# A transformer block in float32: the tensor operations of GpSimd in the MLP phase go to VectorE, and the last tile pair takes three chunk pairs by the classical product

## The chip, the core and the metric

The kernel runs on one core of a Trainium2 chip. The metric is the device time of one execution in microseconds; where several executions are shown, their median counts. Besides the times there is a profile of one execution, taken by the hardware profiler, with a start and a duration for every instruction of every engine: PE (TensorE, matrix products), DVE (VectorE), ACT (ScalarE), POOL (GpSimd) and SP (SyncE, which here only starts transfers). Every engine works through its own queue strictly in the order in which the program was written; a waiting instruction holds up all that stand behind it.

## The reference

A block of a transformer works on 2048 tokens of width 640, in float32:

```python
mod = (silu(c) @ w_mod).reshape(1, 6, 1, 640)          # sa, ca, ga, sb, cb, gb
h = layernorm(x) * (1 + ca) + sa
x = x + ga * attention(h)                              # linear attention, 32 heads of 20
h = layernorm(x) * (1 + cb) + sb
u = h @ w1 + b1                                        # 640 -> 1728
x = x + gb * (max(u, 0) ** 2 @ w2 + b2)                # 1728 -> 640
```

The change concerns the last three lines, the MLP.

## The kernel before

**Numbers in two parts.** TensorE multiplies in a reduced format (`F32R` in the code, `fp32r` in the profile). To keep float32 accuracy every operand is split into a high part (a copy on ScalarE into the reduced format) and a low part (what is left, a subtraction on VectorE, in the helper `lo`, line 87), and a product of two operands takes three matrix products: high by high, high by low, low by high (the helper `three`). So every new operand costs a copy on ScalarE, then a subtraction on VectorE, before its third product can run.

**Tiles and chunks of the MLP.** 16 tiles of 128 tokens form 8 tile pairs, `j` from 0 to 7. The 1728 hidden features are 14 chunks of 128 (the last has 64), which form 7 chunk pairs, `n` from 0 to 6. For each `j` and each `n` there are two half steps. In the first `up(j, 2n)` computes an even chunk of hidden features, in the second `up(j, 2n+1)` the odd one: 15 matrix products into one half of the PSUM bank `UP` (10 for the last chunk). ScalarE applies the relu with the bias (line 1148, tile `ft`), VectorE squares it (line 1149). For the last chunk of 64 features the parts are put together in another way: ScalarE takes one part out of PSUM (line 1152), VectorE adds the other straight from PSUM (`L1153`) and squares (`L1154`). The next `up(j+1, 0)` begins the bank `UP` anew, so it waits until `L1153` has read it.

**The second product, one chunk pair late.** After each `up` stands half of the second product of the chunk pair before (`down(0)`, then `down(1)`), which sums into the PSUM banks `acc`, `acc3x`. The output is cut into 384 columns (left) and 256 columns (right). A chunk pair can be taken in two ways:

- classically (`down_plain`): four blocks of activations (two tiles by two chunks) by two column parts, that is 24 matrix products, 12 of 384 and 12 of 256 columns;
- as a Strassen-Winograd product (`down_pair`): seven block products in place of eight, that is 21 matrix products, 12 of 384 and 9 of 256 columns. It needs sums of the activation blocks (`sums`, four VectorE subtractions and additions of 128x128 on line 1163, split in `split_s` into the tile `rs`) and sums of the weights.

`plain(j, n)` tells which is used: classical for the tile pairs 0 and 1 (`PLAIN`), for the last chunk pair, and for the last two chunk pairs of the last tile pair.

**Sums of the weights.** For the chunk pairs 0 to 5 they are made once, while the tile pairs 1 and 2 run: `t_load` brings two rows of weights (tile `traw`), `t_sums` (line 1225) makes five subtractions, of which two are on GpSimd (128x256 and 128x128) and three on VectorE (128x256), `t_split` splits the results and writes them to memory (`td_a`, `td_b`, `td_c`). From then on `t_fetch` brings them back for every tile pair and chunk pair into the tiles `ring_a`, `ring_b`, `ring_c`; these transfers are started by GpSimd. One of the sums stays in place of the right part of `W2[2n]`; the last tile pair loads and splits the true right part for the chunk pair that it takes classically (`w10_load`, `w10_split`).

**The end of a tile pair.** `first_combos` and `end` put the output `y` together from the banks, `gate` multiplies by `gb`, and `finish` adds the residual `xr` and stores (VectorE and SyncE). The residual is loaded by `residual`, and the bias `bb` (128x640) is added to it by `add_bias` on GpSimd (line 1304), for both tiles of a pair one after the other: in the first chunk pair step of the next tile pair, for pair 1 in the third, for pair 7 in its own sixth. For the last tile pair, GpSimd also adds `xr` to `y` (line 1464) and makes two of the four last additions in `last_downs` (line 1359).

**The next tile pair.** `layer(j+1, at)` runs the layer norm of the next tile pair beside all this, at the half steps in the tables `LN_AT...`: `load_x1` loads two parts (`xm`, `xx`), `add_x` adds them (VectorE, line 974), `ln_pieces` takes mean and variance (ScalarE, with `xx` as scrap space, line 1381), and `t2` transposes on TensorE (`tb`), scales on ScalarE (`hfb`) and splits into `h` on ScalarE and VectorE.

**What sets the order.** For the MLP the order of PE, DVE, ACT and POOL is the order in which the loop is written (`by_hand`). SyncE's transfers are ordered by a scheduler; a transfer waits in SyncE's queue until its source is ready and its target free, and those behind it wait too. The tiles `traw`, `xr`, `xx` share five buffers (`s1`) in rotation, so a load waits for the reader of the tile five loads before.

Of the kernel before, what the change touches and what calls it, by code (L numbers as in the profile page):

```python
# [8 lines left out]
F32 = mybir.dt.float32  # L9
# [29 lines left out]
PLAIN = 2  # L39
W_AT = (  # L40
# [10 lines left out]
def kernel(  # L51
# [1104 lines left out]
    def plain(j, n):  # L1156
        return j < PLAIN or n == NF // 2 - 1 or j == NB - 1 and n == NF // 2 - 2

# [54 lines left out]
    def t_sums(n):  # L1213
# [8 lines left out]
        for eng, o, x, y in ((nc.vector, a[:, l], a[:, r], a[:, l]), (nc.gpsimd, t[:, 1].bitcast(F32), b[:, r], a[:, r]),  # L1222
                             (nc.vector, b[:, r], b[:, r], a[:, l]), (nc.gpsimd, b[:, m], b[:, m], a[:, m]),
                             (nc.vector, b[:, l], b[:, l], b[:, r])):
            eng.tensor_tensor(o, x, y, op=ALU.subtract)
# [17 lines left out]
    def w10_load():  # L1243
        TR_["w10"] = row("s1", "w10")
        f = NF - 4
        nc.sync.dma_start(TR_["w10"][:, R], w2[f * P : (f + 1) * P, R])

    def w10_split():

        t, w = W2[NF - 4][:, :, R], TR_["w10"][:, R]  # L1250
        nc.scalar.activation(t[:, 0], w, AF.Copy)
        lo(t[:, 1], w, t[:, 0])
# [34 lines left out]
    def down_pair(j, n, part):  # L1287
        v, w = W2[2 * n], W2[2 * n + 1]
        last = n == NF // 2 - 2 - (j == NB - 1)
# [12 lines left out]
    def add_bias(j):  # L1302
        for i in range(2):
            nc.gpsimd.tensor_tensor(XR[j, i], XR[j, i], bb, op=ALU.add)
# [39 lines left out]
    def last_downs(j):  # L1344
# [3 lines left out]
        for regs in ((("3", 0, R), ("x", 1, R)), (("2", 0, L),), (("4", 1, L),)):  # L1348
# [4 lines left out]
            for r, i, c in regs:  # L1353
# [4 lines left out]
                eng = nc.gpsimd if r in "x2" else nc.vector  # L1358
                eng.tensor_tensor(Y[j][i][:, c], Y[j][i][:, c], t, op=ALU.add)
# [11 lines left out]
    LN_AT1 = {"load": 3, "add": (5, 5), "ln": (5, 6, 6, 7, 8, 8), 9: (0, 1), 10: (2, 3), 11: (4,)}  # L1371
    LN_AT2 = {"load": 5, "add": (7, 7), "ln": (7, 7, 8, 8, 9, 9), 10: (0, 1), 11: (2, 3), 12: (4,)}
# [42 lines left out]
    for j in range(NB):  # L1415
        for n in range(NP):
# [31 lines left out]
            if n == 3 and j == PLAIN:  # L1448
                finish(j - 1, 0)
            if n == (2 if j > PLAIN else 1) and j:  # L1450
                gate(j - 1, 1)
            if n == (5, 6, 4)[min(j, 2)]:
                residual(j)
            if n == 0 and j and j != PLAIN or n == 5 and j == NB - 1:
                add_bias(j - (n == 0))
            if j == NB - 1 and n == 1:
                w10_load()
            if j == NB - 1 and n == 2:
                w10_split()
            if j == NB - 1 and n == NP - 1:  # L1460
                split_a(j, n, (0,))
                for i in range(2):
                    by_gate(Y[j][i], Y[j][i], slice(0, D))
# [92 lines left out]
```

## Time and profile before

| what | value |
|---|---|
| three executions | 825.34, 829.84, 833.88 us; median 829.84 us |
| the profiled execution, its own time | 825.4 us |
| its span, first to last instruction | 823.7 us |
| mean granted TensorE clock | 0.991 |
| busy: PE, DVE, ACT, POOL | 791.2, 594.4, 443.1, 165.7 us |
| from 420 us to 824 us (the MLP; its first tile pairs run from about there): PE, DVE, POOL busy | 376.5, 264.6, 105.1 us |

TensorE is busy for 96% of the span, so time can only be lost or won where it waits, where its clock is lowered, or in the number of its products. A row of the timeline gives start, duration, engine, line, operation, the tile written and the tile read, and in square brackets how long the engine had been idle and which instruction ended that.

### The profile page before, as it was taken

The page shows a single profiled execution, that of the slowest core. Times are in us where ns is not written, and L with a number is a line of the kernel's source. Part 1 is how long each engine was busy: PE and PEld are TensorE (multiplying, and loading weights), DVE is VectorE, ACT ScalarE, POOL GpSimd, SP SyncE. Part 2 cuts the span into 40 slices and gives each one's busy share as a digit, 9 for nine tenths or more (in the row PEclk, how much of TensorE's full clock was granted, in tenths as well). Part 3 has the DMA queues.
Part 4 walks back from the last instruction along what each step waited for, and adds up shares of the span by engine and source line. Part 5 has one row for each costly group of instructions (what it writes and reads, how often), then busy time and mean ns, then how long its engine had stood idle before and what let it go on. Part 6 is the DMA issues. An engine that isn't in the chain of part 4 may idle for free. (4 is left out here: it accounts for less than half of the span.)

```text
span 823.7 us, 15324 instructions
## 1 busy us (share of the span) xinstructions
PE 791.2 (96%) x5980; PEld 755.1 (92%) x5980; DVE 594.4 (72%) x1017; ACT 443.1 (54%) x987; POOL 165.7 (20%) x294
## 2 busy tenths in 40 slices
PE   9999999999999999999999999968989989899896
PEld 8899999999999888889899998968989989899895
DVE  4499889998777888974176576746767576675766
ACT  4666675567653455565867365344543636436332
POOL 3001201000000214320003020422331223312333
PEclk9999999999999999999999999989999999999999
DMA  8703245433211243131356377694864739556360
GB/s 334 268 33 138 98 130 165 138 102 113 82 49 62 98 149 127 62 112 72 133 197 193 98 259 231 181 305 134 267 191 157 226 99 297 167 169 206 112 192 33
DMA packets 51104, 127.22 MB, mean 154 GB/s; under 512 B 5904, under 2 KB 7056, under 8 KB 51032
## 3 DMA queue, kind: packets, MB, share of 16 engines
q1 hardware_dynamic: 33544, 84.19, 29.9%
q0 software_dynamic: 15184, 36.81, 15.4%
q10 hardware_dynamic: 2304, 5.24, 1.6%
q8 instruction: 47, 0.77, 0.4%
q14 instruction: 25, 0.20, 0.1%
HBM read 96.23 MB, written 29.88 MB: 153 GB/s over the span
## 5 line engine op out<-in xcount | busy, mean ns | idle before, releaser
L77 PE MATMUL up<-h,w 128*128 128x256 f32 x1640 | 212.8, 282 | 16.1 <-DVE ft L1153 11.0
L77 PEld LDWEIGHTS up<-h,w 128*128 128x128 f32 x1640 | 200.8, 191 | 18.9 <-DVE ft L1153 12.0
L1148 ACT ACTIVATE ft<-up,b_t 128x256 f32<-128x256 f32 x104 | 48.7, 468 | 111.2 <-PE up L77 110.7
L77 PE MATMUL acc<-w,ra 128*128 128x384 f32 x446 | 98.3, 341 | 2.0 <-ACT ra L1172 1.5
L1149 DVE TENSOR_TENSOR ft<-ft 128x256 f32<-128x256 f32 x104 | 45.7, 439 | 54.4 <-ACT ft L1148 53.4
L77 PE MATMUL pwo<-wo,ot 128*128 128x256 f32 (+3 forms) x512 | 82.9, 315 | 0.1
L77 PE MATMUL pk<-wk,hT 128*128 128x384 f32 (+1 forms) x480 | 77.2, 312 | 0.9 <-ACT hT L351 0.9
L77 PEld LDWEIGHTS acc<-w,ra 128*128 128x128 f32 x446 | 73.4, 191 | 4.6 <-ACT ra L1172 1.9
L77 PEld LDWEIGHTS pwo<-wo,ot 128*128 128x128 f32 (+1 forms) x512 | 75.5, 188 | 1.9 <-ACT ot L865 0.4
L77 PE MATMUL pq<-wq,hT 128*128 128x384 f32 (+1 forms) x480 | 75.1, 311 | 0.4 <-ACT k L396 0.4
L77 PE MATMUL pv<-wv,hT 128*128 128x384 f32 (+1 forms) x480 | 75.2, 309 | 0.0
L77 PEld LDWEIGHTS pk<-wk,hT 128*128 128x128 f32 x480 | 71.7, 188 | 2.7 <-ACT hT L351 1.1
L77 PEld LDWEIGHTS pq<-wq,hT 128*128 128x128 f32 x480 | 70.7, 188 | 1.5 <-ACT k L396 0.9
L77 PEld LDWEIGHTS pv<-wv,hT 128*128 128x128 f32 x480 | 70.5, 188 | 0.4
L87 DVE TENSOR_TENSOR h<-hfb,h 128x256 fp32r<-128x256 f32 x40 | 32.5, 813 | 49.7 <-ACT h L351 49.6
L87 DVE TENSOR_TENSOR ra<-ft,ra 128x384 fp32r<-128x384 f32 (+2 forms) x85 | 37.7, 463 | 30.1 <-ACT ra L1172 18.6
L1256 POOL DMA_DIRECT2D ring_c<-td_c x35 | 19.0, 542 | 137.4 <-PE acc L77 114.5
L1163 DVE TENSOR_TENSOR ft<-ft 128x128 f32<-128x128 f32 x140 | 42.1, 341 | 1.2
L77 PE MATMUL acc3x<-w,ra 128*128 128x256 f32 x236 | 39.8, 281 | 1.6 <-DVE ra L87 1.6
L1172 ACT ACTIVATE ra<-ft 128x384 fp32r<-128x384 f32 x48 | 25.2, 525 | 29.7 <-DVE ft L1149 29.7
L791 POOL TENSOR_TENSOR dn<-dn,rs_q 128x64 f32<-128x64 f32 x16 | 14.0, 874 | 128.0 <-DVE dn L789 128.0
L77 PEld LDWEIGHTS acc3x<-w,ra 128*128 128x128 f32 x236 | 37.0, 190 | 2.0 <-DVE ra L87 1.8
(244 smaller groups left out, 1451.3 us busy)
## 6 DMA issues: line engine op xcount, KB each, us to landing
ring_c<-td_c POOLq DMA_DIRECT2D x35, 384.0 KB, 3.4
ring_a<-td_a POOLq DMA_DIRECT2D x35, 384.0 KB, 4.7
ring_b<-td_b POOLq DMA_DIRECT2D x35, 256.0 KB, 3.0
esp<-eq SPq DMA_DIRECT2D x12, 640.0 KB, 2.9
el<-esp SPq DMA_DIRECT2D x12, 640.0 KB, 3.9
rw<-in_w SPq DMA_DIRECT2D x23, 320.0 KB, 3.3
wm<-in_w_mod SPq DMA_DIRECT2D x20, 320.0 KB, 3.8
xb<-in_x SPq DMA_DIRECT2D x8, 640.0 KB, 4.1
```

The lines of the kernel that those rows point to most:

```text
L77: nc.tensor.matmul(o, a, b, start=first and i == 0, stop=last and i == len(terms) - 1, skip_group_check=skip,)
L87: (eng or nc.vector).tensor_tensor(out_lo, full, hi.bitcast(F32), op=ALU.subtract)
L791: nc.gpsimd.tensor_tensor(dn, dn, rs, op=ALU.mult)
L1148: nc.scalar.activation(r, p, AF.Relu, bias=b1_t[:, f : f + 1])
L1149: nc.vector.tensor_tensor(r, r, r, op=ALU.mult)
L1163: nc.vector.tensor_tensor(t[:, o], t[:, a], t[:, b], op=op)
L1172: nc.scalar.activation(a[:, 0, :3], t[:, :3], AF.Copy)
L1256: nc.gpsimd.dma_start(RING[j, n, r], TD[n][r].bitcast(F32R))
```

## The change

All tensor operations of GpSimd in the MLP phase, apart from the few of 128x2 elements in the layer norm, go to VectorE; GpSimd is left with the starts of the ring transfers.

- `t_sums` makes all five subtractions on VectorE; for the last chunk pair it stands half a step later, in the middle of the third chunk pair step of tile pair 2.
- `add_bias` is on VectorE and takes one tile at a time. For tile pairs 2 to 7 it stands in the pair's own sixth step, one tile in the middle and one at the end; for pair 0 in the middle of its last step, for pair 1 at the end of pair 2's first step. The residual of the pairs 1 and 3 to 7 is loaded one step earlier.
- `finish` of tile pair 1 moves from the fourth to the second step of pair 2.
- `LN_AT1` (norm of pair 2): chunks 2 and 3 are transposed one half step later, chunk 4 one half step later. `LN_AT2` (norm of pair 3): load and addition one half step earlier.
- The last tile pair takes three chunk pairs classically (`LAST = 3`): it restores two right parts of weights (`plain_load`, `plain_split`) and begins `first_combos` one step earlier; the gate of `y` is one step earlier, the addition of `xr` and all last additions are on VectorE.

In the order of instructions this shows at two places. The first is the end of tile pair 4. GpSimd's queue before has the two bias additions between the ring transfers of the next pair (`ring_0`, the first chunk pair):

```order
L1256 DMA ring_5_b<-td_b 128x512
L1256 DMA ring_0_c<-td_c 128x768
L1256 DMA ring_0_a<-td_a 128x768
L1304 TENSOR_TENSOR xr_4_0_7535<-xr_4_0_7535,bb 128x640
L1304 TENSOR_TENSOR xr_4_1_7537<-xr_4_1_7537,bb 128x640
L1256 DMA ring_0_b<-td_b 128x512
```

VectorE's queue at the same place before, from the squares of chunk 11 on (`h_5` is the next pair's input, `ft_5`, `ra_5`, `rs_5` belong to the chunk pair 5, `ft_6` to the last one):

```order
L87 TENSOR_TENSOR h_5_7521<-hfb_2_7616,h_5_7521 128x256
L87 TENSOR_TENSOR h_5_7521<-hfb_3_7620,h_5_7521 128x256
L1149 TENSOR_TENSOR ft_5_7592<-ft_5_7592 128x256
L87 TENSOR_TENSOR ra_5_7641<-ft_5_7592,ra_5_7641 128x384
L1163 TENSOR_TENSOR ft_5_7592<-ft_5_7592 128x128 x4
L1149 TENSOR_TENSOR ft_6_7677<-ft_6_7677 128x2x128
L87 TENSOR_TENSOR rs_5_7680<-ft_5_7592,rs_5_7680 128x512
L87 TENSOR_TENSOR h_5_7521<-hfb_4_7695,h_5_7521 128x256
L1153 TENSOR_TENSOR ft_6_7677<-up,ft_6_7677 64x256
```

And VectorE's queue there now:

```order
L88 TENSOR_TENSOR h_5_7525<-hfb_3_7620,h_5_7525 128x256
L1309 TENSOR_TENSOR xr_4_0_7447<-xr_4_0_7447,bb 128x640
L1150 TENSOR_TENSOR ft_5_7592<-ft_5_7592 128x256
L88 TENSOR_TENSOR ra_5_7642<-ft_5_7592,ra_5_7642 128x384
L1164 TENSOR_TENSOR ft_5_7592<-ft_5_7592 128x128 x4
L1309 TENSOR_TENSOR xr_4_1_7449<-xr_4_1_7449,bb 128x640
L1150 TENSOR_TENSOR ft_6_7679<-ft_6_7679 128x2x128
L88 TENSOR_TENSOR rs_5_7682<-ft_5_7592,rs_5_7682 128x512
L88 TENSOR_TENSOR h_5_7525<-hfb_4_7697,h_5_7525 128x256
L1154 TENSOR_TENSOR ft_6_7679<-up,ft_6_7679 64x256
```

The two additions have moved from GpSimd's queue into VectorE's, about one step earlier, one ahead of the square of chunk 11 and one ahead of that of chunk 12.

The second place is SyncE's queue in tile pair 2, where the parts `xx` for the norm of pair 3 are loaded. Before:

```order
L1241 DMA td_a<-tst_end 128x768
L1241 DMA td_b<-tst_end 128x512
L1241 DMA td_c<-tst_end 128x768
L970 DMA xx_0_6232<-in_x 128x640
L970 DMA xx_1_6233<-in_x 128x640
L1308 DMA out<-y_0_6025 128x640
```

And now:

```order
L1306 DMA out<-y_0_6025 128x640
L971 DMA xx_0_6181<-in_x 128x640
L1306 DMA out<-y_1_6026 128x640
L971 DMA xx_1_6182<-in_x 128x640
L1241 DMA td_a<-tst_end 128x768
L1241 DMA td_b<-tst_end 128x512
L1241 DMA td_c<-tst_end 128x768
```

The loads of `xx` no longer stand behind the stores of the last weight sums (`tst_end`) but behind the stores of tile pair 1's output, one behind each.

```diff
--- before.py
+++ after.py
@@ -37,6 +37,7 @@
 KEPT = NT - POSTPONED
 W2_AT = 48
 PLAIN = 2
+LAST = 3
 W_AT = (
     *range(21),
     *range(11),
@@ -1154,7 +1155,7 @@
             nc.vector.scalar_tensor_tensor(r[:n], u, 0.0, u, op0=ALU.max, op1=ALU.mult)
 
     def plain(j, n):
-        return j < PLAIN or n == NF // 2 - 1 or j == NB - 1 and n == NF // 2 - 2
+        return j < PLAIN or n == NF // 2 - 1 or j == NB - 1 and n >= NF // 2 - LAST
 
     def sums(j, n):
         t = FT[j, n]
@@ -1219,10 +1220,9 @@
         else:
             t = ring("c" if n % 2 else "b", f"tst{n}_b")[:, :, :256]
         TR_[n, "b"] = t
-        for eng, o, x, y in ((nc.vector, a[:, l], a[:, r], a[:, l]), (nc.gpsimd, t[:, 1].bitcast(F32), b[:, r], a[:, r]),
-                             (nc.vector, b[:, r], b[:, r], a[:, l]), (nc.gpsimd, b[:, m], b[:, m], a[:, m]),
-                             (nc.vector, b[:, l], b[:, l], b[:, r])):
-            eng.tensor_tensor(o, x, y, op=ALU.subtract)
+        for o, x, y in ((a[:, l], a[:, r], a[:, l]), (t[:, 1].bitcast(F32), b[:, r], a[:, r]),
+                        (b[:, r], b[:, r], a[:, l]), (b[:, m], b[:, m], a[:, m]), (b[:, l], b[:, l], b[:, r])):
+            nc.vector.tensor_tensor(o, x, y, op=ALU.subtract)
 
     def t_split(n):
 
@@ -1240,14 +1240,13 @@
             if r:
                 nc.sync.dma_start(TD[n][r], t.bitcast(F32))
 
-    def w10_load():
-        TR_["w10"] = row("s1", "w10")
-        f = NF - 4
-        nc.sync.dma_start(TR_["w10"][:, R], w2[f * P : (f + 1) * P, R])
-
-    def w10_split():
-
-        t, w = W2[NF - 4][:, :, R], TR_["w10"][:, R]
+
+    def plain_load(n):
+        TR_["plain", n] = row("s1", f"w2r_{n}")
+        nc.sync.dma_start(TR_["plain", n][:, R], w2[2 * n * P : (2 * n + 1) * P, R])
+
+    def plain_split(n):
+        t, w = W2[2 * n][:, :, R], TR_["plain", n][:, R]
         nc.scalar.activation(t[:, 0], w, AF.Copy)
         lo(t[:, 1], w, t[:, 0])
 
@@ -1286,7 +1285,7 @@
 
     def down_pair(j, n, part):
         v, w = W2[2 * n], W2[2 * n + 1]
-        last = n == NF // 2 - 2 - (j == NB - 1)
+        last = n == (NF // 2 - 2 if j < NB - 1 else NF // 2 - 1 - LAST)
         if part:
             todo = ("5", S1, RING[j, n, "a"], L), ("6", S2, v, R), ("3", S4, w, R), ("7", S3, RING[j, n, "b"], slice(0, 256))
         else:
@@ -1299,9 +1298,8 @@
             t = XR[j, i] = row("s1", f"xr2_{j}_{i}")
             nc.sync.dma_start(t, X1[j][:, i])
 
-    def add_bias(j):
-        for i in range(2):
-            nc.gpsimd.tensor_tensor(XR[j, i], XR[j, i], bb, op=ALU.add)
+    def add_bias(j, i):
+        add(XR[j, i], XR[j, i], bb)
 
     def store(j, i, a=0, b=D):
         t = 2 * j + i
@@ -1355,8 +1353,7 @@
                 t = u[:, at : at + m] if r != "4" else u[:, :m]
                 at += m
                 by_gate(t, acc(j, r)[1], c)
-                eng = nc.gpsimd if r in "x2" else nc.vector
-                eng.tensor_tensor(Y[j][i][:, c], Y[j][i][:, c], t, op=ALU.add)
+                add(Y[j][i][:, c], Y[j][i][:, c], t)
                 store(j, i, c.start, c.stop)
 
     def prep(n):
@@ -1368,8 +1365,8 @@
     LN2 = {}
 
     LN_AT0 = {"load": 0, "add": (2, 4), "ln": (2, 4, 6, 6, 8, 8), 10: (0, 1), 11: (2, 3), 12: (4,)}
-    LN_AT1 = {"load": 3, "add": (5, 5), "ln": (5, 6, 6, 7, 8, 8), 9: (0, 1), 10: (2, 3), 11: (4,)}
-    LN_AT2 = {"load": 5, "add": (7, 7), "ln": (7, 7, 8, 8, 9, 9), 10: (0, 1), 11: (2, 3), 12: (4,)}
+    LN_AT1 = {"load": 3, "add": (5, 5), "ln": (5, 6, 6, 7, 8, 8), 9: (0, 1), 11: (2, 3), 12: (4,)}
+    LN_AT2 = {"load": 4, "add": (6, 6), "ln": (7, 7, 8, 8, 9, 9), 10: (0, 1), 11: (2, 3), 12: (4,)}
     LN_AT = {"load": 0, "add": (3, 4), "ln": (4, 5, 6, 6, 7, 7), 8: (0, 1), 10: (2, 3), 12: (4,)}
     PREPS = iter([0, 4] * 5 + [0, 1])
 
@@ -1445,23 +1442,30 @@
                 gate(j - 1, 0)
                 if j != PLAIN:
                     finish(j - 1, j < PLAIN)
-            if n == 3 and j == PLAIN:
+            if n == 1 and j == PLAIN:
                 finish(j - 1, 0)
+            if n == 2 and j == PLAIN:
+                t_sums(NP - 2)
             if n == (2 if j > PLAIN else 1) and j:
                 gate(j - 1, 1)
-            if n == (5, 6, 4)[min(j, 2)]:
+            if n == (5, 5, 4, 3)[min(j, 3)]:
                 residual(j)
-            if n == 0 and j and j != PLAIN or n == 5 and j == NB - 1:
-                add_bias(j - (n == 0))
+            for i in range(2):
+                if n == 6 and j == 0 or n == 5 and j >= PLAIN and i == 0:
+                    add_bias(j, i)
             if j == NB - 1 and n == 1:
-                w10_load()
-            if j == NB - 1 and n == 2:
-                w10_split()
+                for k in range(NP - LAST, NP - 1):
+                    plain_load(k)
+            if j == NB - 1 and n == 3:
+                for k in range(NP - LAST, NP - 1):
+                    plain_split(k)
+            if j == NB - 1 and n == NP - 2:
+                for i in range(2):
+                    by_gate(Y[j][i], Y[j][i], slice(0, D))
             if j == NB - 1 and n == NP - 1:
                 split_a(j, n, (0,))
                 for i in range(2):
-                    by_gate(Y[j][i], Y[j][i], slice(0, D))
-                    nc.gpsimd.tensor_tensor(Y[j][i], Y[j][i], XR[j, i], op=ALU.add)
+                    add(Y[j][i], Y[j][i], XR[j, i])
             up(j, 2 * n + 1)
             if j >= PLAIN and n == 0:
                 down(1)
@@ -1474,11 +1478,10 @@
                 t_fetch(j, n, "b")
             if m == NP + 1:
                 t_split(NP - 2)
-                add_bias(j - 1)
             prep(next(PREPS, 0))
             if n == 0 and j:
                 end(j - 1, "x", 1, R)
-            if n == (2 if j > PLAIN else 3 if j == PLAIN else 0) and j:
+            if n == (2 if j > PLAIN else 1 if j == PLAIN else 0) and j:
                 finish(j - 1, j >= PLAIN)
             layer(j + 1, 2 * n + 1)
             if 0 <= m < NP - 2:
@@ -1487,9 +1490,12 @@
                 t_split(m - 1)
             if 0 < m + 1 < NP - 1:
                 t_load(m + 1)
-            if m == NP:
-                t_sums(m - 2)
-            if j == NB - 1 and n == NP - 2:
+            if m == NP - 1:
+                for i in range(2):
+                    add_bias(j - 1, i)
+            if j >= PLAIN and n == 5:
+                add_bias(j, 1)
+            if j == NB - 1 and n == NP - LAST:
                 first_combos(j)
             prev = j, n
     last_downs(NB - 1)
```

## The prediction

> **What bounds the kernel now.** I read the page's first part, then the list of what TensorE waited for in the MLP, then the timeline around each of these waits, and last the granted clock behind them. The page gives the span and TensorE's busy time:
>
> ```profile
> span 823.7 us, 15324 instructions
> PE 791.2 (96%) x5980; PEld 755.1 (92%) x5980; DVE 594.4 (72%) x1017; ACT 443.1 (54%) x987; POOL 165.7 (20%) x294
> ```
>
> TensorE is the bound, and 32.5 us of the span are not covered by it. The list of its waits from 420 us on names where (line and releaser, then total us, times, longest):
>
> ```profile
> PE up L77 <- DVE ft L1153: 11.0, 5, 2.2
> PE up L77 <- ACT ft L1148: 5.0, 1, 5.0
> PE acc3x L77 <- DVE ra L87: 1.6, 1, 1.6
> PE acc L77 <- ACT ra L1172: 1.5, 2, 1.3
> PE acc L77 <- DVE rs L87: 1.3, 1, 1.3
> PE acc L77 <- ACT rs L1188: 0.9, 2, 0.5
> ```
>
> These six rows hold 21.3 us, nearly all of it behind work of VectorE. The question is whether VectorE is late because it has too much to do. The timeline at the end of tile pair 4, from chunk 11 on, answers it (start, duration, engine):
>
> ```profile
> 656.63 0.42 DVE L87 TENSOR_TENSOR h<-hfb,h 128x256 fp32r<-128x256 f32 x1 [1.08 <-ACT h L351]
> 656.99 0.42 DVE L1149 TENSOR_TENSOR ft<-ft 128x256 f32<-128x256 f32 x1
> 658.01 0.56 DVE L87 TENSOR_TENSOR ra<-ft,ra 128x384 fp32r<-128x384 f32 x1 [0.59 <-ACT ra L1172]
> 658.85 1.20 PE L77 MATMUL acc<-w,ra 128*128 128x384 f32 x6
> ...
> 661.93 3.47 DVE L87 TENSOR_TENSOR h<-hfb,h 128x256 fp32r<-128x256 f32 x1 [1.04 <-ACT h L351]
> 662.01 0.47 ACT L1152 ACTIVATE ft<-up,b_t 64x256 f32<-64x256 f32 x1
> 662.04 3.07 POOL L1304 TENSOR_TENSOR xr<-xr,bb 128x640 f32<-128x640 f32 x2
> ...
> 665.32 0.41 DVE L1153 TENSOR_TENSOR ft<-up,ft 64x256 f32<-64x256 f32 x1
> ```
>
> The same VectorE subtraction into `h` takes 0.42 us at 656.6 and 3.47 us at 661.9. In between stand GpSimd's two bias additions, 3.07 us; the subtraction ends at 665.40, 0.3 us after them. So VectorE does not compute longer, it is held for as long as GpSimd works on tensors. L1153 stands behind the held instruction, and the next pair's first `up` waits for L1153. The five waits of 11.0 us are this one place at the end of tile pairs 2 to 6; the first products of the next pairs stand in these rows:
>
> ```profile
> 567.63 1.99 PE L77 MATMUL up<-h,w 128*128 128x256 f32 x15 [2.06 <-DVE ft L1153]
> 616.62 1.99 PE L77 MATMUL up<-h,w 128*128 128x256 f32 x15 [2.24 <-DVE ft L1153]
> 665.78 3.19 PE L77 MATMUL up<-h,w 128*128 128x256 f32 x15 [2.24 <-DVE ft L1153]
> 716.34 2.63 PE L77 MATMUL up<-h,w 128*128 128x256 f32 x15 [2.24 <-DVE ft L1153]
> 766.96 1.99 PE L77 MATMUL up<-h,w 128*128 128x256 f32 x15 [2.24 <-DVE ft L1153]
> ```
>
> **The change part by part.**
>
> *The five waits.* With GpSimd's additions gone the subtraction at 661.93 would end at 662.35. L1153 also needs ScalarE's L1152, done at 662.48, and would end near 662.9. TensorE becomes free at 665.78 − 2.24 = 663.54. So nothing is late there any more: −11.0 us.
>
> *The clock behind them.* The same 15 products take 1.99 us in three of the rows and 3.19 and 2.63 us in two. The windows at these two show why; the number behind POOL's is the granted clock:
>
> ```profile
> 665.70:669.00 3.30, 3.21 (x16) 3.22 (x17) 1.27 (x5) 0.42 (x1) 0.00 (x0) 0.59 0.41 108
> 719.00:722.00 3.00, 3.00 (x15) 3.00 (x15) 2.33 (x6) 1.02 (x3) 0.00 (x0) 0.69 0.00 0
> ```
>
> The distances of the five starts are 48.99, 49.16, 50.56 and 50.62 us: behind the third and the fourth wait a pair took 1.57 and 1.63 us more, behind the second 0.17. Both times the lowered clock stands right behind a wait, so without the waits I take these 3.4 us off as well. The Trainium skill (TensorE: Matmul & The Clock Gate, the section on the clock gate) says that the clock is halved after an idle window of about 3.4 us; by that rule a wait of 2.24 us should not lower it, the 3.4 us would have another cause and stay, and the forecast below would be 806 us instead of 803; two of the five waits were followed by it in this trace, which goes against the rule.
>
> *Tile pair 2.* Two stalls lie here: 0.4 + 1.3 us for `rs`, and 5.0 us for the relu of an `up`.
>
> ```profile
> 529.75 4.29 DVE L1163 TENSOR_TENSOR ft<-ft 128x128 f32<-128x128 f32 x4
> 530.25 3.10 POOL L1304 TENSOR_TENSOR xr<-xr,bb 128x640 f32<-128x640 f32 x2
> 536.11 2.56 SPq L970 DMA_DIRECT2D xx<-in_x  x2
> ...
> 544.18 0.82 DVE L974 TENSOR_TENSOR xm<-xm,xx 128x640 f32<-128x640 f32 x1 [1.18 <-DMA xx<-in_x]
> 545.83 0.46 ACT L1148 ACTIVATE ft<-up,b_t 128x256 f32<-128x256 f32 x1
> 546.34 3.57 PE L77 MATMUL up<-h,w 128*128 128x256 f32 x15 [4.97 <-ACT ft L1148]
> ```
>
> The four activation sums take 4.29 us under GpSimd's additions, against 1.0 us elsewhere (four of the L1163 price below). Behind them stand the low parts of the last weight sums, behind these in SyncE's queue the loads of `xx`; they start at 536.1, and the second addition waits for its load until 544.18. ScalarE's pass over `xx` stands ahead of the relu at 545.83, and TensorE waits for that. Now the loads stand behind the two stores of pair 1's output, whose `finish` moves two steps up. Counted in half steps of 3.3 us (a pair's 48.99 − 2.24 us over 14), the later load starts about three half steps, 10 us, before 536.1; the 8 us that it took here then end near 534, where the addition now stands, half a step earlier. Gone: 0.4 + 1.3 + 5.0 us, and the slow 15 products behind the long wait (3.57 against 1.99, 1.6 us): −8.3 us. What is late next here is a third product for `rs`, by 0.1 us: VectorE's bias additions for pair 1 stand ahead of its low part.
>
> *Tile pair 1 and the end.*
>
> ```profile
> 504.45 1.03 PE L77 MATMUL acc<-w,ra 128*128 128x384 f32 x3 [1.32 <-ACT ra L1172]
> ...
> 805.40 1.17 PE L77 MATMUL acc<-ring_a,rs 128*128 128x384 f32 x3 [0.50 <-ACT rs L1188]
> 812.15 3.61 POOL L1464 TENSOR_TENSOR y<-y,xr 128x640 f32<-128x640 f32 x2 [8.15 <-DVE y L1314]
> 816.11 0.74 PE L77 MATMUL acc3x<-w,ra 128*128 128x256 f32 x4 [1.55 <-DVE ra L87]
> ```
>
> The copy into `ra` at 504.45 was late because ScalarE had the transposed chunks of the next pair ahead of it; these now come half a step later, behind it: −1.3 us. At the end, GpSimd's last bias additions cost 0.5 us of waiting and 0.5 us in the stretched products at 805.40 (1.17 against about 0.68): −1.0. The 1.55 us at 816.11 is VectorE held by 3.61 us of GpSimd's additions. Their replacements stand ahead of L1153 and make it about 0.2 us late: −1.4.
>
> *What is added.* The prices on VectorE and TensorE (a subtraction of 128x256 is the 0.42 us shown above):
>
> ```profile
> L1311 DVE TENSOR_TENSOR y<-y,xr 128x640 f32<-128x640 f32 x14 | 11.5, 820 | 0.5
> L1163 DVE TENSOR_TENSOR ft<-ft x140: 276/285/3562, 517.3 to 804.4; 128x128 f32<-128x128 f32 x140
> 649.09 0.51 PE L77 MATMUL acc<-w,rs 128*128 128x256 f32 x3
> 649.43 0.50 PE L77 MATMUL acc3x<-w,rs 128*128 128x256 f32 x3
> ```
>
> VectorE gets 16 bias additions of 0.82 us, six pairs of weight sums of 0.42 + 0.28 us, and in pair 7 two additions of 0.82 and two last ones (0.4 and 0.55 us): 13.1 + 4.2 + 1.6 + 1.0 = 19.9 us. None of it is new waiting as long as a half step of 3.3 us has room. The one place where it hasn't is ahead of the square of chunk 11. Pushed from 656.99 to about 657.9, it moves ScalarE's copy to 658.95 and `ra`'s low part to 659.5. TensorE wanted the copy at 658.85 and the low part two products later, at 659.2: 0.36 us late. That is five tile pairs (2 to 6; pair 7 has no `h`) by 0.36 = +1.8 us. From below it is nothing, from above both additions of five pairs in full, 5 x 1.64 = 8.2 us. The second addition stands ahead of the square of chunk 12, which waits for its relu anyway, so I take the first alone. For pair 0 the two additions delay the last chunk's `ra`: +0.1.
>
> The third classical chunk pair is 24 products for 21; three of 256 columns start 0.34 us apart in the rows above, so +0.34. It drops one set of activation sums, three ring transfers and one split. The second restored weight part is one copy of 0.4 and one subtraction of 0.42 us in a step with 3 us to spare. The last two additions on VectorE run behind one another instead of beside each other: +0.3, at most 1.0, with nothing after them but the last store.
>
> *Sum.* 11.0 + 3.4 + 8.3 + 1.3 + 1.0 + 1.4 = 26.4 off; 1.8 + 0.1 + 0.1 + 0.3 + 0.3 = 2.6 on; 23.8 us net. The profiled execution took 825.4 us, so 801.6 us. It is the fastest of the runs shown (825.3, 829.8, 833.9), 4.4 below their median. Had all five waits been followed by 1.6 us of lowered clock, three more would make it 830.2: most of that scatter can come from the waits that go. So I add 1.4 us, not 4.4: **803 us**.
>
> **The rivals.**
>
> *The wait in pair 2 stays* (0.12). The loads of `xx` now stand behind two stores, each of which waits for a `finish`; if one slips, the 5.0 us and their 1.6 us of clock return: 810 us. Against it speaks the distance of 10 us.
>
> *The moved work is late* (0.13). If both bias additions of a pair come out in full (8.2 instead of 1.8) and the five weight sums of six chunk pairs as well (4.2): 803 + 10.6 = 814 us. For it speaks that VectorE works strictly in order; against it that it was busy for 72% of the span, held time included. In the Trainium skill, Perfetto Trace Analysis (Optimizing Scalar/DVE Operations) allows moving work from a saturated VectorE to GpSimd; with the 19.9 us all on the path in place of the 1.8, the result would be 821 us by it. The same section doubts its own advice because the two share a read port, and the 3.47 us row bears out the doubt.
>
> *The lowered clock has another cause* (0.04). Three of the five waits were not followed by it; if the two were chance, the 3.4 us stay: 803 + 3.4 = 806 us.
>
> *GpSimd is not what holds VectorE* (0.05). Then the long subtraction only happens to lie there, the waits stay, and the time is within 1%, 822 to 832 us. Against it speak three places with the same picture, each as long as GpSimd's work.
>
> *Slower: the ring comes late* (0.03). GpSimd starts the ring transfers, and VectorE's additions could hold GpSimd as GpSimd's held VectorE. These rows are a transfer's start, and the products that read it:
>
> ```profile
> 653.94 0.53 POOL L1256 DMA_DIRECT2D ring_c<-td_c  x1 [2.73 <-PE acc L77]
> 659.88 0.69 PE L77 MATMUL acc<-ring_c,ra 128*128 128x384 f32 x3
> ring_c<-td_c POOLq DMA_DIRECT2D x35, 384.0 KB, 3.4
> ```
>
> A transfer lands 3.4 us after its start, 2.5 us before its use. Every one of the 34 chunk pairs left would have to come 3.5 us later, one us past its use, to take back the 23.8 us and 8 more: 837 us. A start took 0.53 us beside a busy VectorE all along, so this is unlikely.
>
> **How the numbers follow.** Forecast 0.63, from 797 (no new wait, 2.6 us less, and a run like the fastest) to 808; the others as given. A range of 797 to 813 us leaves out the upper half of the moved work, GpSimd's innocence and the slower case, about 0.17. A measurement of this kernel tells about 1% from no change, that is 821.5 and 838.1 us. Faster: 0.63 + 0.12 + 0.13 + 0.04 = 0.92, less 0.01 for the far end of the second rival; within 1%: 0.06; slower: 0.03.
>
> **What would show it.** Right: no VectorE row of `h` or L1163 over 1 us in the MLP; no wait of an `up` for L1153; no wait for the relu in pair 2; granted clock 1.00 through the MLP; distances of the pairs' starts near 47.1 us (48.99 − 2.24 + 0.36). The 0.36 us shows as a wait of `acc` for `ra` once in each of pairs 2 to 6. Wrong: VectorE's rows stay long with GpSimd idle; waits for `xx`; or products waiting for `ring` transfers.

## The result and the profile after

The changed kernel takes 801.87 us (median of 4 runs, 800.62 to 803.07), the kernel before beside it 830.02 us (4 runs, 825.34 to 833.88): a ratio of 0.966, 95% interval 0.961 to 0.972. The profiled execution took 801.5 us, 23.9 less than that of before. The page's first part:

```profile
span 799.8 us, 15255 instructions
PE 786.2 (98%) x5983; PEld 750.7 (94%) x5983; DVE 580.0 (73%) x1046; ACT 443.7 (55%) x988; POOL 127.8 (16%) x259
```

VectorE got 29 instructions more and is busy 14.4 us less: the time in which it was held counted as busy (the 3.47 us subtraction of before is one such row). What TensorE waits for from 420 us on is now this whole list (line and releaser, then total us, times, longest):

```profile
PE acc L78 <- DMA ring_c<-td_c: 2.1, 3, 0.9
PE acc L78 <- DMA ring_a<-td_a: 1.1, 1, 1.1
PE up L78 <- ACT ft L1149: 0.4, 1, 0.4
```

Of the waits for VectorE nothing is left; new are waits for ring transfers and a short one for a relu. The end of tile pair 4 in the timeline (start, duration), the place that the prediction showed of before:

```profile
644.25 0.82 DVE L1309 TENSOR_TENSOR xr<-xr,bb 128x640 f32<-128x640 f32 x1
...
646.00 0.56 DVE L88 TENSOR_TENSOR ra<-ft,ra 128x384 fp32r<-128x384 f32 x1 [0.59 <-ACT ra L1173]
646.17 1.41 PE L78 MATMUL acc<-w,ra 128*128 128x384 f32 x6
...
649.47 0.42 DVE L88 TENSOR_TENSOR h<-hfb,h 128x256 fp32r<-128x256 f32 x1 [0.31 <-ACT h L352]
...
650.05 0.42 DVE L1154 TENSOR_TENSOR ft<-up,ft 64x256 f32<-64x256 f32 x1 [0.15 <-ACT ft L1153]
...
650.92 1.86 PE L78 MATMUL up<-h,w 128*128 128x256 f32 x15
```

The subtraction into `h` is back at 0.42 us, L1154 (L1153 before) ends 0.45 us ahead of the next pair's first product, and that product comes without a wait and at full clock (15 products in 1.86 us).

The last `up` of each pair, 10 products, marks the stretches in both timelines. The first and the last of the eight, after and then before:

```profile
453.63 1.42 PE L78 MATMUL up<-h,w 128*128 128x256 f32 x10
...
788.41 1.30 PE L78 MATMUL up<-h,w 128*128 128x256 f32 x10
```

```profile
455.47 1.43 PE L77 MATMUL up<-h,w 128*128 128x256 f32 x10
...
810.85 1.30 PE L77 MATMUL up<-h,w 128*128 128x256 f32 x10
```

| stretch, from one such row to the next | before | after | gain | by the prediction's terms |
|---|---|---|---|---|
| start to pair 0 | 455.47 | 453.63 | 1.8 | -0.1 |
| pair 1 | 51.06 | 48.89 | 2.2 | 1.3 |
| pair 2 | 56.08 | 50.76 | 5.3 | 7.8 |
| pair 3 | 48.77 | 46.92 | 1.9 | 1.7 |
| pair 4 | 49.16 | 47.88 | 1.3 | 2.1 |
| pair 5 | 50.56 | 47.91 | 2.6 | 3.5 |
| pair 6 | 50.62 | 46.63 | 4.0 | 3.5 |
| pair 7 | 49.13 | 45.79 | 3.3 | 2.9 |
| to the end of the span | 12.85 | 11.39 | 1.5 | 1.1 |
| sum | 823.7 | 799.8 | 23.9 | 23.8 |

The sum is right to 0.1 us. Its parts are not: pair 2 gained 2.5 us less than its terms and the first two stretches 2.8 us more, and they cancel.

### The profile page after: what moved, and what is told of

The parts are those of the page before. It is cut to its first block, busy times and chain, and to the rows that moved or that the text cites. A ratio compares the mean times of both kernels' runs of the same rounds, so it can differ in the third digit from the quotient of the medians.

```text
span 799.8 us, 15255 instructions
## 1 busy us (share of the span) xinstructions
PE 786.2 (98%) x5983; PEld 750.7 (94%) x5983; DVE 580.0 (73%) x1046; ACT 443.7 (55%) x988; POOL 127.8 (16%) x259
## 4 chain that ended last, share of the span: by engine, by line
PE 80%; DVE 9%; ACT 4%; DMA 3%; POOL 2%; issue 1%; ACTq 0%; POOLq 0%; DVEq 0%
PE up L78 20%; PE acc L78 15%; PE pk L78 8%; PE pq L78 7%; PE pv L78 7%; PE pwo L78 7%; PE acc3x L78 4%; PE kvp L421 2%; DMA ring_c<-td_c 2%; DVE dn L790 2%; DVE scr L788 2%; PE te L829 2%; DMA ring_a<-td_a 1%; PE tb L340 1%; PE ta L340 1%
## 5 line engine op out<-in xcount | busy, mean ns | idle before, releaser
L78 PE MATMUL up<-h,w 128*128 128x256 f32 x1640 | 208.9, 279 | 0.4 <-ACT ft L1149 0.4
L78 PEld LDWEIGHTS up<-h,w 128*128 128x128 f32 x1640 | 197.8, 188 | 2.0 <-ACT ft L1149 1.8
L1150 DVE TENSOR_TENSOR ft<-ft 128x256 f32<-128x256 f32 x104 | 44.0, 423 | 52.9 <-ACT ft L1149 52.1
L88 DVE TENSOR_TENSOR h<-hfb,h 128x256 fp32r<-128x256 f32 x40 | 17.0, 425 | 48.1 <-ACT h L352 48.0
L1164 DVE TENSOR_TENSOR ft<-ft 128x128 f32<-128x128 f32 x136 | 33.3, 286 | 1.2
```

The lines of the kernel that those rows point to most:

```text
L78: nc.tensor.matmul(o, a, b, start=first and i == 0, stop=last and i == len(terms) - 1, skip_group_check=skip,)
L88: (eng or nc.vector).tensor_tensor(out_lo, full, hi.bitcast(F32), op=ALU.subtract)
L1150: nc.vector.tensor_tensor(r, r, r, op=ALU.mult)
L1164: nc.vector.tensor_tensor(t[:, o], t[:, a], t[:, b], op=op)
```

## The experiments

### Is it GpSimd that holds VectorE?

To the changed kernel, two additions on GpSimd at the old place. They read two constants and write the transposed activations of the pair that is done, which nobody reads any more:

```diff
+            if n == 0 and j > PLAIN:
+                dead = H2[j - 1].rearrange("p d s n -> p (d s n)")[:, :D]
+                for i in range(2):
+                    nc.gpsimd.tensor_tensor(dead, gb_b, bb, op=ALU.add)
```

> The changed kernel, and in it two additions on GpSimd at the end of each of the tile pairs 2 to 6, where the kernel before had its bias additions: 128x640, two operands from SBUF, the result into a dead buffer, so that no work of another engine waits for them. VectorE's work stays as in the changed kernel. My theory (GpSimd's tensor work holds VectorE): the subtraction into h at the end of the pair takes over 3 us instead of 0.42, L1154 ends near 653.3 instead of 650.5 in pair 4, and TensorE waits about 2.3 us at each of five ends: 802 + 11.5 = 813 us, up to 821 if all five are followed by 1.6 us of lowered clock. Rival (GpSimd is innocent, the gain came from the other half steps): 801 to 803 us and a subtraction of 0.42 us.

Measured: 808.91 us (808.35 to 809.43). The end of pair 4 in its timeline:

```profile
653.58 1.99 DVE L88 TENSOR_TENSOR h<-hfb,h 128x256 fp32r<-128x256 f32 x1 [0.30 <-ACT h L352]
653.69 3.29 POOL L1454 TENSOR_TENSOR h<-gb_b,bb 128x640 fp32r<-128x640 f32 x2
655.49 0.41 DVE L1154 TENSOR_TENSOR ft<-up,ft 64x256 f32<-64x256 f32 x1
655.93 1.33 DVE L1155 SCALAR_TENSOR_TENSOR ft<-ft 64x256 f32<-64x256 f32 x1
```

VectorE's own work is that of the changed kernel, so GpSimd does hold it; but for 2 us, not 3.5, and the time lies between what the two theories gave. The subtraction ends 0.23 us after GpSimd's first addition (3.29 / 2 behind 653.69), not after the second. L1154, with one operand in PSUM, runs in its usual 0.41 us while the second addition is under way; L1155, with both operands in SBUF, is held until that one ends. Four of the five ends show the same durations to 0.01 us. TensorE waited at most 0.8 us at an end instead of 2.2. So the hold here is by instruction, and it goes by the operands of the instruction that is held, as far as these rows tell. In the kernel before the two additions wrote two buffers; here both write the same. The next run lets the second write elsewhere (`dead` is the whole buffer there):

```diff
-                    nc.gpsimd.tensor_tensor(dead, gb_b, bb, op=ALU.add)
+                    nc.gpsimd.tensor_tensor(dead[:, i * D : (i + 1) * D], gb_b, bb, op=ALU.add)
```

> As the first run with two additions on GpSimd (808.9 us, VectorE's subtraction held 1.99 us, that is through the first of the two only), with one difference: the second addition writes into another part of the dead buffer, so that it needn't come after the first one's write, as in the kernel before, where the two wrote two buffers. My theory (two additions without a gap hold VectorE through both): the subtraction takes 3.2 to 3.5 us, TensorE waits about 2.2 us at each of five ends, 813 us, and up to 821 if the lowered clock follows each. Rival (one instruction of GpSimd holds VectorE at a time, whatever follows): 808 to 810 us and 1.99 us as before. Of the lowered clock I expect it behind one to three of five waits above 2 us.

Measured: 820.21 us (817.55 to 821.44), 18.3 us above the changed kernel's 801.87. The old picture is back, the subtraction to the hundredth:

```profile
659.89 3.47 DVE L88 TENSOR_TENSOR h<-hfb,h 128x256 fp32r<-128x256 f32 x1 [0.31 <-ACT h L352]
659.99 3.07 POOL L1454 TENSOR_TENSOR h<-gb_b,bb 128x640 fp32r<-128x640 f32 x2
```

Two additions that needn't wait for each other hold VectorE through both. The first products of pairs 3 to 7 in this run:

```profile
559.56 3.32 PE L78 MATMUL up<-h,w 128*128 128x256 f32 x15 [0.57 <-DVE ft L1154]
...
611.10 3.55 PE L78 MATMUL up<-h,w 128*128 128x256 f32 x15 [2.24 <-DVE ft L1154]
...
663.74 2.03 PE L78 MATMUL up<-h,w 128*128 128x256 f32 x15 [2.29 <-DVE ft L1154]
...
714.27 1.99 PE L78 MATMUL up<-h,w 128*128 128x256 f32 x15 [2.25 <-DVE ft L1154]
...
763.60 2.71 PE L78 MATMUL up<-h,w 128*128 128x256 f32 x15 [2.24 <-DVE ft L1154]
```

Four of the waits are 2.2 to 2.3 us again, and the lowered clock comes back with them: the first, second and fifth of these groups are slow, the third and fourth are not (the first stands behind two waits, 1.37 us for `rs` and 0.57 us, 3.5 us from the one's start to the other's end).

Does it matter what GpSimd does? Two more runs at the same place, with operations of one operand, and with five that only write:

```diff
-                    nc.gpsimd.tensor_tensor(dead, gb_b, bb, op=ALU.add)
+                    nc.gpsimd.tensor_scalar(dead, bb, 2.0, None, op0=ALU.mult)
```

> As the run with two additions on GpSimd, but two operations of one operand each (a row times 2.0, 128x640). If what counts is that GpSimd reads SBUF, VectorE is held for as long as these take, which may be less than 1.57 us each: 804 to 815 us, with the subtraction into h as long as both. If only operations with two operands hold VectorE: 801 to 803 us.

```diff
-                for i in range(2):
-                    nc.gpsimd.tensor_tensor(dead, gb_b, bb, op=ALU.add)
+                for i in range(5):
+                    nc.gpsimd.memset(dead.bitcast(F32), 0.0)
```

> As the run with two additions on GpSimd, but five operations that write 128x640 zeros and read nothing; the one such operation of 64x640 in the trace takes 0.63 us, so about 3 us in all. The Trainium skill (SBUF - State Buffer) says that VectorE with two SBUF operands is in conflict only with a GpSimd operation that reads SBUF. By that rule: 801 to 803 us and a subtraction of 0.42 us. If any tensor work of GpSimd holds VectorE: about 813 us, as with the additions. I hold the first for likelier (0.7).

Measured: 805.08 us (803.92 to 806.74) and 804.24 us (803.36 to 805.56). The end of pair 4 with one operand, then with none:

```profile
651.86 1.14 DVE L88 TENSOR_TENSOR h<-hfb,h 128x256 fp32r<-128x256 f32 x1 [0.30 <-ACT h L352]
651.97 3.89 POOL L1454 TENSOR_SCALAR h<-bb 128x640 fp32r<-128x640 f32 x2
```

```profile
652.82 0.43 DVE L88 TENSOR_TENSOR h<-hfb,h 128x256 fp32r<-128x256 f32 x1 [0.30 <-ACT h L352]
652.90 3.42 POOL L1454 MEMSET h<- 128x640 f32 x5
```

Writing holds nothing: 0.43 us beside 3.42 us of GpSimd's work. The Trainium skill (SBUF — State Buffer, SBUF: two separate sides) says that a VectorE operation with two SBUF inputs is in conflict only with a GpSimd operation that reads SBUF, and the runs agree. It also says that the loser is blocked for the whole instruction: with two operands the trace agrees, with one it doesn't. There the subtraction took 1.14 us and ended 0.9 us ahead of GpSimd's first operation (3.89 / 2 behind 651.97, if the profile's times for GpSimd hold); neither of my two expectations had that. No `up` waits for L1154 in either run. Both are 2 to 3 us above 801.87 all the same, and their lists show longer waits for the ring, 5.0 and 6.0 us instead of 3.2. That the added work makes the ring late, because each third transfer stands behind it in GpSimd's queue, is not shown: a second measurement of the changed kernel, in the last group of runs below, gave 803.73 us with 6.3 us of such waits and without the added work.

### Engine or half step?

The kernel before, with nothing but its bias additions on VectorE, at the old half steps:

```diff
-            nc.gpsimd.tensor_tensor(XR[j, i], XR[j, i], bb, op=ALU.add)
+            nc.vector.tensor_tensor(XR[j, i], XR[j, i], bb, op=ALU.add)
```

> The kernel before with one edit: its bias additions run on VectorE, at the old half steps (the weight sums and the last additions stay on GpSimd). My theory: the five waits (11.0), the clock behind them (3.4), the wait for rs in pair 2 (1.7) and 1.0 in pair 7 go; the relu wait of pair 2 (5.0 + 1.6) and that of pair 1 (1.3) stay, and both additions stand ahead of chunk 1's square, where they cost between nothing and 1.6 us in six pairs: 808 to 816 us, 811 the likeliest. Rival (the half steps decide, not the engine): above 818 us.

Measured: 809.25 us (808.85 to 810.40), beside 830.87 of before. This one line brings 21.6 of the 28 us between the medians. The two additions in their old place, and what is left in pair 2:

```profile
665.04 1.55 DVE L1304 TENSOR_TENSOR xr<-xr,bb 128x640 f32<-128x640 f32 x2
...
667.61 1.56 PE L77 MATMUL acc<-w,ra 128*128 128x384 f32 x6
```

```profile
542.62 3.57 PE L77 MATMUL up<-h,w 128*128 128x256 f32 x15 [4.47 <-ACT ft L1148]
```

TensorE has no wait behind the additions there; the six products take 1.56 us instead of 1.20, 0.36 us for each of five pairs. What the rest of the change had still to gain is this, the wait of 4.47 us with its slow products, and 1.3 and 1.7 us of waits in pair 1 and at the end.

The other way round: the changed kernel with its bias additions on GpSimd, at the new half steps:

```diff
-        add(XR[j, i], XR[j, i], bb)
+        nc.gpsimd.tensor_tensor(XR[j, i], XR[j, i], bb, op=ALU.add)
```

> The changed kernel with one edit: the bias additions go back to GpSimd, but stay at the new half steps. My theory (GpSimd's additions hold VectorE wherever they stand, and what it costs goes by what stands behind the held instruction): they now run behind the starts of ring_a and ring_b of the sixth chunk pair; a low part of ra or a copy is held by up to 1.2 us, TensorE waits 0 to 1 us at each of two places in six pairs: 803 to 808 us. Rival (the new half steps alone do it, whichever engine adds): 801 to 803 us.

Measured: 819.40 us (816.27 to 819.57), beside 803.73 of the changed kernel on the same chip. The direction was expected, the size wasn't: 15.7 us more, where at most 6 were expected. The end of pair 4:

```profile
648.93 1.77 DVE L88 TENSOR_TENSOR h<-hfb,h 128x256 fp32r<-128x256 f32 x1 [1.24 <-ACT h L352]
...
651.78 2.15 DVE L88 TENSOR_TENSOR h<-hfb,h 128x256 fp32r<-128x256 f32 x1 [1.08 <-ACT h L352]
652.05 1.59 POOL L1302 TENSOR_TENSOR xr<-xr,bb 128x640 f32<-128x640 f32 x1
652.17 1.98 PE L78 MATMUL up<-h,w 128*128 128x256 f32 x15 [1.12 <-ACT ft L1149]
...
654.88 1.56 PE L78 MATMUL acc<-w,ra 128*128 128x384 f32 x6 [0.72 <-ACT ra L1173]
```

Both subtractions into `h` are held, not only the low part of `ra` as I had worked out. ScalarE's next pass waits for the first of them, the relu stands behind that pass, and the square and the copy behind the second: the two holds cost TensorE waits of 1.12 and 0.72 us, and the six products behind the second take 1.56 us instead of 1.20. At the same half steps VectorE's additions cost 0.2 us (1.41 instead of 1.20).

The same question for the weight sums (the edit is shown in part):

```diff
-            nc.vector.tensor_tensor(o, x, y, op=ALU.subtract)
+            eng.tensor_tensor(o, x, y, op=ALU.subtract)  # eng: nc.gpsimd for the second and the fourth
```

> The changed kernel with one edit: two of the five weight sums of each chunk pair go back to GpSimd. In the kernel before they took 0.75 to 0.85 and 0.6 us. My theory: VectorE is held by up to 0.8 us at each of six places in pairs 1 and 2, half of them where something waits for it: 802 to 805 us. Rival (VectorE with all five sums is what is late): 799 to 801 us.

Measured: 805.40 us (803.86 to 811.39), beside 803.73 (802.62 to 804.42): too near to call. VectorE is held here too (0.81 and 0.93 us for operations of 0.42), but TensorE's list has no wait behind these places. The weight sums' part of the change is not shown to matter.

### Pair 2 and the end

The changed kernel with the old order in pair 2 (finish of pair 1 in the fourth step, loads and additions of `xx` half a step later; the edit is shown in part, the second tile's `finish` moves likewise):

```diff
-    LN_AT2 = {"load": 4, "add": (6, 6), ...
+    LN_AT2 = {"load": 5, "add": (7, 7), ...
-            if n == 1 and j == PLAIN:
+            if n == 3 and j == PLAIN:
                 finish(j - 1, 0)
```

> The changed kernel with the old steps for the output of pair 1 and for the loads of xx in pair 2: finish in the fourth step, loads at half step 5, additions at 7. SyncE's queue then has the order of the kernel before: the last weight parts' stores, xx, then the output. All sums stay on VectorE, not held. My theory (the order of SyncE's queue makes xx late): xx is started near 529, lands 6 to 8 us later, VectorE waits for it 2 to 4 us at half step 7 and a relu in pair 2 comes 1 to 4 us late: 804 to 807 us. Rival (in the kernel before only the held sums made it late): 801 to 803 us, and no wait for xx.

Measured: 806.41 us (805.07 to 808.32). The loads, the second addition and the late `up`:

```profile
529.36 1.72 SPq L971 DMA_DIRECT2D xx<-in_x  x2
...
536.54 0.79 PE L78 MATMUL acc<-ring_c,ra 128*128 128x384 f32 x3 [1.42 <-DMA ring_c<-td_c]
...
537.40 0.83 DVE L975 TENSOR_TENSOR xm<-xm,xx 128x640 f32<-128x640 f32 x1 [2.03 <-DMA xx<-in_x]
...
539.55 2.72 PE L78 MATMUL up<-h,w 128*128 128x256 f32 x15 [2.22 <-ACT ft L1149]
```

As expected, the loads start at 529.4, VectorE waits 2.0 us for `xx`, and the relu is 2.2 us late, behind a ring wait of 1.4 us that already took a part of it. So the order of SyncE's queue carries the wait. The held sums do so for a small part only: in the run with VectorE's bias additions at the old half steps the four sums behind which the loads stand take 1.02 us instead of 4.29, the loads start 26.0 us behind the last `up` of pair 1 (531.3 and 505.3) instead of 29.6, and the wait is still 4.5 us instead of 5.0. That it shrinks by so little because a held VectorE makes TensorE late as well is my reading, not shown.

The changed kernel with two classical chunk pairs in the last tile pair, and the gate in the last step again, as it has to be then (the edit is shown in part, without the gate's lines):

```diff
-LAST = 3
+LAST = 2
```

> The changed kernel with two classical chunk pairs in the last tile pair instead of three; the multiplication by the gate goes back to the last step. By my sum the third one costs 0.3 us of products and saves nothing that is waited for: 801 to 802 us. Rival (the third one is what removes the 1.55 us wait and the 1.0 us in pair 7): 803 to 804.5 us, with a wait of the last products for ra or rs.

Measured: 806.25 us (805.66 to 806.70), 4.4 above the 801.87 and 2.5 above the second measurement of the changed kernel (803.73, on another chip). Both ranges were too low; by the second distance the rival's 1 to 2.6 us more was right. VectorE's queue at the end, and TensorE behind it:

```profile
791.16 0.82 DVE L1312 TENSOR_TENSOR y<-y,gb_b 128x640 f32<-128x640 f32 x1
...
793.61 0.82 DVE L1309 TENSOR_TENSOR y<-y,xr 128x640 f32<-128x640 f32 x1
794.35 0.41 DVE L1154 TENSOR_TENSOR ft<-up,ft 64x256 f32<-64x256 f32 x1
...
796.16 0.74 PE L78 MATMUL acc3x<-w,ra 128*128 128x256 f32 x4 [2.45 <-DVE ra L88]
```

Two multiplications by the gate and two additions, 3.3 us, stand ahead of L1154. With three classical pairs the gate's two are done a step earlier, because `first_combos` can be. The third classical pair, which I had booked at +0.3 us for its products, is what lets the wait of 2.45 us go at the end. The rest of the distance is not settled: this run's list has 4.7 us of ring waits, and the changed kernel's own vary from 3.2 to 6.3.

### The ring

In the changed kernel's timeline the ring waits stand here, and beside the first two SyncE starts the loads of `xx` for a pair that is not yet due:

```profile
535.94 0.79 PE L78 MATMUL acc<-ring_c,ra 128*128 128x384 f32 x3 [0.85 <-DMA ring_c<-td_c]
...
535.97 1.15 SPq L971 DMA_DIRECT2D xx<-in_x  x2
...
539.59 0.77 PE L78 MATMUL acc<-ring_a,rs 128*128 128x384 f32 x3 [1.14 <-DMA ring_a<-td_a]
...
626.21 0.80 PE L78 MATMUL acc<-ring_c,ra 128*128 128x384 f32 x3 [0.57 <-DMA ring_c<-td_c]
...
680.98 0.79 PE L78 MATMUL acc<-ring_c,ra 128*128 128x384 f32 x3 [0.67 <-DMA ring_c<-td_c]
```

The window of the first two shows the DMA engines busy throughout (behind TensorE's busy time the granted clock, the share of the DMA engines and GB/s):

```profile
535.00:540.00 5.00, 3.00 (x21) 1.00 1.06 349
```

A full window alone does not make the ring late: from 580 to 585 us the share is 1.03 and no product waits. In pair 4 the loads start at 626.52, after the wait, so they can't be its cause. These loads run as soon as a buffer is free, half a pair or more ahead of their use. GpSimd has room now, so it starts them for pairs 4 to 7, one step into the pair before, behind its `ring_b` (the edit is shown in part; SyncE no longer starts these loads):

```diff
+        if j > PLAIN + 1 and at == 1:
+            load_xx(j)  # nc.gpsimd.dma_start(XX[j][i], x[t * P : (t + 1) * P])
```

> The changed kernel, with the loads of xx for tile pairs 4 to 7 started by GpSimd behind its first ring_b of the pair before, instead of by SyncE as soon as a buffer is free, where they run beside the output's store, the load of xr and the ring transfers. My theory (the ring waits of the changed kernel, 0.85 + 1.14 us in pair 2, 0.57 in pair 4, 0.67 in pair 5, come from this crowding): 1 to 2.5 us faster than the changed kernel, 799.5 to 801 us, with no ring wait in pairs 4 and 5. Rival (GpSimd's own queue is what is slow, and two more transfers in it make the ring later): 802.5 to 805 us.

> The kernel with the loads of xx on GpSimd's queue once more, in more rounds: 799.5 to 801.5 us, 1 to 2.5 us below the changed kernel of the same call, if the crowding of transfers is what made the ring late; if the 800.2 us was chance, no difference.

> The changed kernel once more, beside the run that moves the loads of xx: 800.5 to 803.5 us. Both theories expect the same; it gives the distance on the same chip.

Measured: 800.17 us (800.02 to 802.42), and in more rounds 801.73 (799.20 to 803.78) beside 803.73 (802.62 to 804.42) of the changed kernel on the same chip. Of its two profiles the first has 2.3 us of ring waits and none from pair 3 on, the second 3.5 us with one of 1.10 us in pair 4; the changed kernel's two have 3.2 and 6.3. It is about 2 us faster than the changed kernel and the fastest of all, but the ranges overlap: likely, not shown. That crowding makes the ring late is borne out by the first profile alone; ring waits that differ by 3.1 us between two profiles of the same program are larger than the effect.

## Why the prediction was right, point by point

- **The five waits (11.0 us).** Right, and shown both ways: one line on another engine takes them away, two additions with nobody waiting for their result bring four of them back at 2.2 to 2.3 us. "Held for as long as GpSimd works on tensors" was too wide. Operations with two operands hold it to their end, those with one delay it (1.14 us), those that only write do nothing (0.43 us); and of VectorE's instructions that ran beside an addition, L1154 with one operand in PSUM was not held.
- **The clock behind them (3.4 us).** Right. It is 1.00 throughout the changed kernel's MLP and falls again in the runs that wait: behind two waits of 2.24 us and a pair of shorter ones in one run, behind waits of 4.47, 2.45, 2.22 and 2.15 us in four others, and behind a pair of 0.66 and 1.47 us in the second run with the loads on GpSimd's queue (15 products in 3.26 us, clock 0.66). Like waits of 2.11, 2.25 and 2.29 us were not followed by it. What decides between them is open. The Trainium skill's idle window of about 3.4 us (TensorE: Matmul & The Clock Gate, the section on the clock gate) is more than any of these waits but the one of 4.47 us.
- **Pair 2 (8.3 us, 7.8 with what is added there).** Mis-sized: its stretch gained 5.3. The relu wait and the wait for `rs` went, as worked out. In their place came ring waits of 0.85 and 1.14 us and 0.4 us for a relu, 2.4 of the missing 2.5 us. The prediction had the ring only as a rival that must come late in every chunk pair; a little late, in a stretch where the share of the DMA engines was 1.06, was not in the sum.
- **The additions ahead of chunk 11's square (1.8 us).** Mis-sized: no wait of `acc` for `ra`, only six products in 1.41 us instead of 1.20, so 0.2 us per pair and 1.0 in all. Pairs 3 and 6, without ring waits, gained 0.2 and 0.5 us more than the terms; pairs 4 and 5, with ring waits of 0.57 and 0.67, about 0.8 less. The distances were to be near 47.1 us; for pairs 3 to 6 they are 46.6 to 47.9.
- **Pairs 0 and 1 (0.1 on, 1.3 off).** Missed: 4.0 us came off up to the end of pair 1. Near pair 0's end the trace of before has GpSimd's two bias additions and a held VectorE as well, here the square, and I didn't look there:

```profile
448.32 3.27 POOL L1304 TENSOR_TENSOR xr<-xr,bb 128x640 f32<-128x640 f32 x2 [11.92 <-DVE h L87]
...
450.10 1.77 DVE L1149 TENSOR_TENSOR ft<-ft 128x256 f32<-128x256 f32 x1
...
452.49 0.62 PE L77 MATMUL acc<-w,ra 128*128 128x384 f32 x2 [0.17 <-ACT ra L1172]
```

  The square takes 1.77 us instead of 0.42, and the products behind it come late by small waits (0.2 to 0.3 us each) and run stretched, 1.4 us in all; two of these waits are the smallest rows of the list of waits, which the prediction does not show. With the 0.4 us by which the two runs already differed ahead of it, this is the 1.8 us of the first stretch. Of pair 1's 2.2 us the prediction had 1.3; the cause of the other 0.9 stays open.
- **The last tile pair and the end (1.0 + 1.4 off, 0.3 + 0.3 on).** The sum was right, 4.8 us gained with the last wait against 4.0 by the terms. The reason for the third classical pair was not: I priced its products and didn't see that the 1.4 us hang on it.
- **The 1.4 us for a run like the fastest** were not needed: the median lies 0.4 us from the profiled run, and in the second measurement 2 us higher, about where the 803 was.

So the main term, which carries the sign and most of the size, was right and is shown by the runs. That the total came out to 1 us is luck: a ring that was late (3.2 us and its products) and pairs 0 and 1 that were better (2.8 us) cancelled. One small sum of the prediction is off as well: the chances outside its range (half of 0.13, 0.05 and 0.03) add up to about 0.15, not 0.17.

## What to carry to other kernels

When one engine's instruction takes a multiple of its usual time, look at what the other engines run in just that stretch before deciding that it has too much to do; here a single line moved from an "idle" GpSimd to the "busy" VectorE was worth 21.6 us and took VectorE's busy time down from 594.4 to 582.6 us. Work that GpSimd is to keep beside VectorE should write without reading (0.43 us beside it), or read one operand rather than two (1.14 against 1.99 or 3.47). And once the waits for an engine are gone, look at the stretches where the DMA engines are busy throughout: here the longest of the waits that are left stood in one of them.

## What the runs showed of the hardware that I had not expected

- A GpSimd addition of two SBUF operands held a VectorE subtraction of two SBUF operands to its own end; two such additions into separate buffers held it through both (3.47 us), two into the same buffer let it through between them (1.99 us).
- A VectorE operation with one operand in PSUM ran in its usual 0.41 us beside GpSimd's second addition, while the one behind it with two SBUF operands was held to 1.33, at four ends alike.
- Five GpSimd writes of 128x640, 0.64 us each, left VectorE at 0.43 us; a one-operand operation slowed it to 1.14 without holding it to its end.
- The lowered clock (0.62 to 0.71 over windows of 4 or 5 us) followed waits of 2.15, 2.22, 2.24, 2.45 and 4.47 us, and once waits of 0.66 and 1.47 us close together, and not others of 2.11, 2.25 and 2.29 us.
